# Where a segment's normalised features are made: after the previous segment's last projection, or between its matmuls

## The chip, the cores and the metric

The kernel runs on one core of a Trainium2 chip. A core has five engines with a queue each: TensorE (PE, matrix products; the profile lists its weight loads as PEld), VectorE (DVE), ScalarE (ACT), GpSimd (POOL), and SyncE (SP), which here only issues DMAs. Each engine works through its own queue in order and waits on semaphores for the others. The metric is device time in microseconds (us); smaller is better.

## The reference

The reference is one transformer block with a conditioning vector, in float32. `c` gives six rows of 512 values through `silu(c) @ w_mod`: shift, scale and gate for the attention half, and the same for the feed-forward half.

```
x = A_x                                       # 2048 x 512
h = layernorm(x) * (1 + ca) + sa
x = x + ga * A(h)
h = layernorm(x) * (1 + cb) + sb
x = x + gb * ((h @ w_gate) * (h @ w_up)) @ w_down
```

`A` is attention with 32 heads of 16 and a compressive memory. The 2048 rows are four segments of 512. Inside a segment it is a softmax over the keys at or before the query, with `q = h @ wq`, `k = h @ wk`, `v = h @ wv`. Beside it each head keeps a 16x16 memory `M` and a vector `z` of all earlier segments: the answer of the memory is `phi(q) M / phi(q) z`, with `phi(t) = t + 1` above zero and `exp(t)` below; it is mixed with the softmax part by `sigmoid(beta)`, and after each segment `M` and `z` take in `phi(k)` and `v`. The output goes through `wo`.

## The kernel before

**Numbers as pairs.** Products of float32 matrices are made of three passes: each operand is split into a high part `H` and a low part `L` (what is left over), and PE adds up HH, LH and HL. The splitting costs ACT a copy and another engine a subtraction for every tile.

**The features of a segment.** `ln` (lines 207 to 231) turns the 512 rows of a segment, four tiles `xt[0..3]` of 128 rows, into four column blocks `d = 0..3`, each 128 x 512. It is a generator, and is advanced step by step by whoever calls it. Its steps are, for segments after the first:

- four row steps of `ln_rows` (line 167): `bn_stats` and `bn_aggr` on DVE, one row tile each;
- one step for the reciprocal root: Ln and Exp on ACT (lines 181, 183) and five small operations on POOL (lines 187 to 191);
- four row steps that subtract the mean and multiply, one row tile each, on DVE;
- four feature steps, one per column block: four transposes on PE into a PSUM bank (tile `atp`), ACT scales and shifts that into `ahf` (line 205) and copies it to `ahH` (line 222), POOL subtracts to get `ahL` (line 223). After the second and the fourth of them the generator yields `False`.

**The projections.** `a_kq(s, g, nm)` (line 747) makes keys or queries of one group of eight heads (g = 0..3) of segment s: twelve matmuls into one PSUM bank (`kps` or `qps`), in four quarters of three, quarter k reading feature block k. It yields after each quarter. After the last quarter ACT takes the bank out (`kf`, `qf`, line 765); a chain on ACT and POOL then splits it into three bfloat16 parts (lines 770 to 780) and SP writes them to HBM. Where the memory needs phi, two more ACT passes follow (lines 801, 802).

**The loop and the fill.** From line 1113 a loop runs over 32 units v (four heads of a segment each) in five slots. A slot puts, in this order, into the queues: `q_step` (two PE banks of logits, whose maxima DVE takes), in slot 1 `av_step` (32 matmuls `tb`), then the fill, then `k_step` (logits again, into the one bank pair `lk`, which ACT turns into exponentials, line 330, and POOL masks, line 333). The fill is the work of other stages: the projections, the features, the memory. `fill_a` (line 955) gives its order. PE's instructions are chained in program order, and so are DVE's in the loop; DVE and ACT work that calls `pin` stands behind the PE instruction before it.

How much fill goes into a slot is counted in credit (line 1044): each of the slots 0, 2, 3 and 4 adds 0.25 x 5.8 = 1.45 (5.2 from unit 20 on), slot 1 adds nothing; a quarter of a projection takes 0.68, a feature step 0.45, a row step nothing, a memory step 0.5 or 0.9. The slot's fill ends when the credit is no longer above zero. A `False` ends the slot's fill at once, and what credit is left stays for the next slot.

**Who advances `ln`.** For the next segment, `fill_a` loads the four row tiles at g = 2 (line 975) and weaves the steps of `ln` into the projections of g = 2 and g = 3 (lines 977 to 980). `weave(a, b, at)` (line 669) advances b after the yields of a whose numbers are in `at`: 0, 1, 2 are after the first three quarters, 3 is after the last, with the bank already being emptied or, for queries of later segments, at the first waiting step of the memory. What `ln` has not done by then is done in one go at line 963, before the next segment's first keys.

**Buffers.** Projections and transposes share two PSUM banks (tag "ms"). High and low parts of the features have eight buffers in all, just those of one segment; `ahf` has three. The queries of g = 3 are the last readers of a segment's features: their quarter k is the last use of block k.

Of the kernel before, what the change touches and what calls it, by code (L numbers as in the profile page):

```python
# [58 lines left out]
def tile_kernel(ctx, tc, x, wq, wk_, wv, wo, beta, w_gate, w_up, w_down, c, w_mod, out):  # L59
# [29 lines left out]
    def MM(*a, **k):  # L89
        return pe(nc.tensor.matmul(*a, **k))  # L90
# [12 lines left out]
    def pst(shape, tag, name, dt=F32):  # L103
        tg, n = TAGS[tag]
        return psp.tile(list(shape), dt, tag=tg, name=name, bufs=n)
# [4 lines left out]
    def bank(name, dt=F32, shape=(P, 512)):  # L110

        nbank[0] += 1
        return pst(shape, btag[nbank[0] % len(btag)], name, dt)
# [53 lines left out]
    def ln_rows(pool, xt, s, pfx):  # L167

        first = pfx == "a" and s == 0
        V, A = (CV, CA) if first else (vec, act)  # L170
        mv = pool.tile([P, 4, 2], F32, tag="mv", name=f"{pfx}mv{s}", bufs=2)
        for t in range(4):
            st = pool.tile([P, 6], F32, tag="st", name=f"{pfx}st{s}_{t}", bufs=2)
            i = V.bn_stats(st, xt[t])
            if not first:
                pin(i)
            V.bn_aggr(mv[:, t, :], st)
            if not first:
                yield 0.0
        sd = pool.tile([P, 4], F32, tag="sd", name=f"{pfx}sd{s}", bufs=2)  # L180
        A.activation(sd, mv[:, :, 1], AF.Ln, bias=epst[:, 0:1])
        y = pool.tile([P, 4], F32, tag="y", name=f"{pfx}y{s}", bufs=2)
        A.activation(y, sd, AF.Exp, scale=-0.5)
        a = pool.tile([P, 4], F32, tag="ya", name=f"{pfx}ya{s}", bufs=2)
        b = pool.tile([P, 4], F32, tag="yb", name=f"{pfx}yb{s}", bufs=2)
        eng = CV if first else nc.gpsimd
        eng.tensor_mul(a, y, y)
        eng.tensor_scalar(b, mv[:, :, 1], 1.0, EPS, op0=ALU.mult, op1=ALU.add)
        eng.tensor_mul(b, b, a)
        eng.tensor_scalar(b, b, -0.5, 1.5, op0=ALU.mult, op1=ALU.add)  # L190
        eng.tensor_mul(y, y, b)
        yield 0.0
        for t in range(4):
            i = V.tensor_scalar(xt[t], xt[t], mv[:, t, 0:1], y[:, t:t + 1],
                                op0=ALU.subtract, op1=ALU.mult)
            if not first:
                pin(i)
                yield 0.0
        if first:
            yield 0.0  # L200

    def ln_col(ps, h, xt, d, sc, sh, A):
        for t in range(4):
            TP(ps[:, t * P:(t + 1) * P], xt[t][:, d * P:(d + 1) * P], ident)
        A.activation(h, ps, AF.Identity, scale=sc[:, d:d + 1], bias=sh[:, d:d + 1])

    def ln(pool, hpool, xt, s, sc, sh, pfx, hb, fast, kept_h=None):

        first = pfx == "a" and s == 0
        V, A = (CV, CA) if first else (vec, act)  # L210
        yield from ln_rows(pool, xt, s, pfx)
        hH, hL = [], []
        for d in range(KT):
            h = pool.tile([P, L], F32, tag="hf", name=f"{pfx}hf{s}_{d}", bufs=hb[2])
            ln_col(bank(f"{pfx}tp{s}_{d}"), h, xt, d, sc, sh, A)
            hi = hpool.tile([P, L], F32R, tag=hb[0].format(d), name=f"{pfx}hH{s}_{d}", bufs=hb[1])
            lo = hpool.tile([P, L], F32R, tag=hb[0].format(4 + d), name=f"{pfx}hL{s}_{d}", bufs=hb[1])
            if fast:
                V.tensor_copy(hi, h)
                V.tensor_sub(lo, h, hi.bitcast(F32))  # L220
            else:
                act.activation(hi, h, AF.Copy)
                nc.gpsimd.tensor_sub(lo, h, hi.bitcast(F32))  # L223
            hH.append(hi)
            hL.append(lo)
            if kept_h is not None:
                kept_h.append(h)
            yield 0.45
            if not first and d % 2 == 1:
                yield False  # L230
        return hH, hL

# [37 lines left out]
    def q_step(u, i):  # L270

        Q, K = qst[u % NB], kst[u % NB]
        if i == 0:
            nms[u] = ap.tile([P, 16], F32, tag="nm", name=f"nm{u}", bufs=2)
        nm = nms[u]
        for b in range(2):
# [7 lines left out]
            for hh, qb in parts:  # L284
                n = (qb + 1) * P
                MM(qp[:, c:c + n], Q[0:96, hh, qb * P:(qb + 1) * P], K[0:96, hh, 0:n], start=True, stop=True)
                c += n
# [14 lines left out]
    def n_step(u):  # L302

        Q = qst[u % NB]
        tp = pst([32, P], "tb", f"ntp{u}", BF)
# [3 lines left out]
        for i in range(2):  # L309
            nc.scalar.dma_start(Q[96 + i:97 + i].rearrange("p h (q t) -> p (h q) t", t=P), nt[16 * i:16 * i + 16])  # L310

    def k_step(u, i):

        Q, K = qst[u % NB], kst[u % NB]
        kp = psp.tile([P, 2, 512], F32, tag="lk", name=f"k{u}_{i}", bufs=1)

        def mm(b, c, h, kb):
            MM(kp[:, b, c:c + L - kb * P], K[:, h, kb * P:(kb + 1) * P], Q[:, h, kb * P:], start=True, stop=True)

# [240 lines left out]
    def load_mod(i):  # L560
        r = []
        for k in range(KT):
            a = pa.tile([P, 512], F32, tag="x", name=f"wm{i}_{k}", bufs=4)
            nc.sync.dma_start(a, wm[:, k, i * D:(i + 1) * D])
            r.append(a)
        return r
# [102 lines left out]
    def weave(a, b, at):  # L669

        i = 0
        for w in a:
            yield w
            if w:
                for _ in range(at.count(i)):
                    w = next(b, None)
                    if w or w is False:
                        yield w
                i += 1
# [275 lines left out]
    def fill_a():  # L955
        for w in w2:
            next(w)
        yield from av
        memq.extend((a_mem(0, 0), a_mem(0, 1)))
        lns = None  # L960
        for s in range(NSEG):
            if s > 0:
                hcur[0] = yield from lns
                if s < 3:
                    r = load_mod(2 * s)
            for g in range(2 if s == 0 else 0, NG):
                ws = []
                if s == 0 and g < 3:
                    ws = [load_g(nm, w, g + 1) for nm, w in (("k", wk_), ("q", wq))]
                for w in ws:  # L970
                    next(w)
                K, Q = a_kq(s, g, "k"), a_kq(s, g, "q")
                if g >= 2 and s + 1 < NSEG:
                    if g == 2:
                        xts[s + 1] = xload(s + 1)
                        lns = a_ln(s + 1)
                        Q = weave(Q, lns, (0, 1, 2, 3) if s > 0 else (2, 3))
                    else:
                        K = weave(K, lns, (0, 2) if s > 0 else (0, 1, 2, 3))
                        Q = weave(Q, lns, (0, 1, 2))  # L980
                if g == 1 and 0 < s < 3:
                    acc = mod_acc(r)
                    K, Q = weave(K, acc, (0, 2)), weave(Q, acc, (0, 2))
                if s == NSEG - 1 and g == 1:
                    xr0 = xr_load(0, pa, (0, 1), "x")
                    ready = chain(wo_weights(), wo_op(0, None, B["orl"], us[0]))
                if s == NSEG - 1 and 0 < g < NG - 1:
                    K, Q = weave(K, ready, (0, 1, 2, 3)), weave(Q, ready, (0, 1, 2, 3))
                if s == NSEG - 1 and g == NG - 1:
                    yield from weave(Q, ready, (0, 1, 2, 3))  # L990
                    memq.append(a_mem(s, g))
                    yield from K
                    yield from ready
                    yield from wo_mm(0, us[0], xr0, (0, 1))
                    break
                yield from K
                for w in ws:
                    next(w)
                yield from Q
                if s > 0 and g == 0:  # L1000
                    while vfree[0] < s:
                        yield None
                    if s < 3:
                        yield from weave(a_v(s), mod_acc(r), (1, 3, 5, 7))
                        yield from a_mod(2 * s, r[0])
                        r = load_mod(2 * s + 1)
                    else:
                        yield from a_v(s)
                        B["orl"] = wo_load(0, wpool)
                if g == 1 and 0 < s < 3:  # L1010
                    yield from a_mod(2 * s + 1, r[0])
                memq.append(a_mem(s, g))
        while memq or memt:
            yield mem_step() or 0.0
            yield False
# [283 lines left out]
    for q in range(2):  # L1299
# [98 lines left out]
        for m in range(2):  # L1398
            s = 2 * q + m
# [111 lines left out]
```

## Time and profile before

| | us |
|---|---|
| three timed runs | 879.31, 879.39, 883.21 |
| their median | 879.39 |
| the profiled execution's own time | 881.91 |
| span in that execution, first to last instruction | 879.8 |
| PE busy | 832.8 |
| DVE busy | 650.6 |
| ACT busy | 472.5 |
| POOL busy | 424.1 |

The loop over the 32 units fills about the span from 40 to 500 us; what comes after is the feed-forward half. The three places where one segment's features are made for the next lie at about 80, 195 and 315 us. In a timeline row stand the start, the time from start to end of what is merged in the row, the engine, the line, the operation, its output and inputs, shapes and count; a bracket at the end gives the idle time of the engine before it and what ended it. PE's matmuls overlap, so the distance from one start to the next says more than a length. PE's line is mostly L90, a helper that records every matmul, so one goes by tile names: `k`, `q`, `tb` are the attention, `kps` and `qps` the projections, `atp` the transposes of the features.

### The profile page before, as it was taken

The page shows a single profiled execution, that of the slowest core. Times are in us where ns is not written, and L with a number is a line of the kernel's source. Part 1 is how long each engine was busy: PE and PEld are TensorE (multiplying, and loading weights), DVE is VectorE, ACT ScalarE, POOL GpSimd, SP SyncE. Part 2 cuts the span into 40 slices and gives each one's busy share as a digit, 9 for nine tenths or more (in the row PEclk, how much of TensorE's full clock was granted, in tenths as well). Part 3 has the DMA queues.
Part 4 walks back from the last instruction along what each step waited for, and adds up shares of the span by engine and source line. Part 5 has one row for each costly group of instructions (what it writes and reads, how often), then busy time and mean ns, then how long its engine had stood idle before and what let it go on. Part 6 is the DMA issues. An engine that isn't in the chain of part 4 may idle for free.

```text
span 879.8 us, 14406 instructions
## 1 busy us (share of the span) xinstructions
PE 832.8 (95%) x4824; PEld 583.0 (66%) x4824; DVE 650.6 (74%) x1728; ACT 472.5 (54%) x740; POOL 424.1 (48%) x564
## 2 busy tenths in 40 slices
PE   8998999989999989999978899999999999999998
PEld 5765565555565656655644567788778888887886
DVE  7697677986778868788888759898784856666532
ACT  3757667777677766777554664333363523333321
POOL 4545546546455665486352533987200846550000
PEclk9999899999999999999999999999999999999999
DMA  7774456665648665677695552543414232212032
GB/s 236 225 235 159 146 160 201 214 209 174 207 142 252 199 190 157 220 234 239 209 285 177 160 180 97 176 146 105 163 30 127 87 120 64 56 55 93 0 118 96
DMA packets 112667, 139.46 MB, mean 159 GB/s; under 512 B 20112, under 2 KB 71312, under 8 KB 112592
## 3 DMA queue, kind: packets, MB, share of 16 engines
q1 hardware_dynamic: 106368, 130.91, 48.7%
q10 hardware_dynamic: 6224, 7.62, 2.4%
q8 instruction: 38, 0.62, 0.3%
q14 instruction: 37, 0.30, 0.1%
HBM read 87.48 MB, written 50.76 MB: 157 GB/s over the span
## 4 chain that ended last, share of the span: by engine, by line
PE 66%; DVE 13%; DMA 8%; ACT 5%; POOL 4%; issue 3%; ACTq 1%; SPq 0%; POOLq 0%; DVEq 0%
PE g L90 23%; PE acc L90 14%; PE tb L90 5%; DVE q L40 5%; PE k L90 5%; PE q L90 5%; PE vps L90 4%; PE kps L90 3%; PE qps L90 2%; ACT pt L330 2%; DMA xr<-in_x_dram 2%; PE wops L90 2%; POOL ahL L223 1%; DVE x L40 1%; DVE nm L40 1%
## 5 line engine op out<-in xcount | busy, mean ns | idle before, releaser
L40 DVE CUSTOM_DVE_ANT_0 q<-q,cmask 128x384 f32<-128x384 f32 (+3 forms) x512 | 246.7, 508 | 66.4 <-PE q L90 56.4
L330 ACT ACTIVATE pt<-k 128x1024 f32<-128x1024 f32 x160 | 163.8, 1024 | 68.7 <-PE k L90 47.3
L333 POOL TENSOR_SCALAR_AFFINE_SELECT pt<-pt 128x256 f32<-128x256 f32 (+1 forms) x224 | 105.4, 484 | 174.3 <-ACT pt L330 173.9
L90 PE MATMUL q<-kst,qst 96*128 96x384 bf16 (+3 forms) x512 | 102.1, 301 | 11.7 <-DVE nm L40 10.4
L90 PE MATMUL k<-qst,kst 98*128 98x384 bf16 (+3 forms) x512 | 97.9, 303 | 11.6 <-ACT pt L330 10.7
L448 POOL TENSOR_TENSOR w<-w 128x256 f32<-128x256 f32 (+1 forms) x84 | 72.0, 869 | 55.7 <-DMA w<-in_w_up_dram 38.2
L443 POOL TENSOR_TENSOR AL<-w,AH 128x512 fp32r<-128x512 f32 (+1 forms) x42 | 58.2, 1388 | 48.0 <-ACT AH L439 46.8
L90 PE MATMUL tb<-pt,v 128*32 128x512 f32 (+3 forms) x1024 | 76.2, 438 | 0.2 <-POOL pt L333 0.2
L90 PEld LDWEIGHTS <-kst 98*128 98x128 bf16 x512 | 38.8, 99 | 56.6 <-issue 48.4
L40 DVE DVE_READ_ACCUMULATOR2_ANT nm<- 128x1 f32 x512 | 72.3, 141 | 0.0
L90 PEld LDWEIGHTS <-qst 96*128 96x128 bf16 x512 | 43.6, 98 | 39.1 <-issue 14.4
L439 ACT ACTIVATE AH<-w 128x512 fp32r<-128x512 f32 (+3 forms) x88 | 46.8, 565 | 33.6 <-POOL w L448 20.5
L1453 DVE TENSOR_TENSOR mL<-mid,mH 128x512 fp32r<-128x512 f32 (+1 forms) x44 | 32.9, 751 | 41.4 <-ACT mH L1452 39.4
L90 PE MATMUL acc<-DH,mL 128*128 128x512 f32 x144 | 56.6, 393 | 0.9 <-DVE mL L1453 0.9
L90 PE MATMUL acc<-DH,mH 128*128 128x512 f32 x144 | 57.2, 397 | 0.0
L90 PE MATMUL acc<-DL,mH 128*128 128x512 f32 x144 | 56.5, 393 | 0.0
L90 PEld LDWEIGHTS tb<-pt,v 128*32 128x32 f32 x1024 | 28.7, 110 | 39.5 <-issue 35.9
L1452 ACT ACTIVATE mH<-mid 128x512 fp32r<-128x512 f32 (+1 forms) x44 | 27.1, 627 | 51.7 <-PE acc L90 50.1
L1245 ACT ACTIVATE p<-g 128x512 f32<-128x512 f32 (+1 forms) x22 | 13.1, 597 | 73.2 <-PE g L90 73.1
L443 DVE TENSOR_TENSOR AL<-w,AH 128x512 fp32r<-128x512 f32 (+3 forms) x44 | 29.2, 671 | 19.1 <-ACT AH L439 18.2
L359 ACT ACTIVATE tsb<-tb 128x512 f32<-128x512 f32 x32 | 19.1, 596 | 35.0 <-PE tb L90 33.4
L90 PE MATMUL g<-chH,AH 128*128 128x512 f32 (+1 forms) x88 | 34.8, 395 | 0.7 <-ACT p L1245 0.7
(286 smaller groups left out, 2060.1 us busy)
## 6 DMA issues: line engine op xcount, KB each, us to landing
kst<-kd SPq DMA_DIRECT2D x32, 384.0 KB
qst<-qd SPq DMA_DIRECT2D x32, 384.0 KB
td<-tsb ACTq DMA_DIRECT2D x28, 256.0 KB
wm<-in_w_mod_dram SPq DMA_DIRECT2D x24, 256.0 KB
kd<-k SPq DMA_DIRECT2D x16, 384.0 KB
qd<-q SPq DMA_DIRECT2D x16, 384.0 KB
w<-in_w_gate_dram SPq DMA_DIRECT2D x40, 128.0 KB
w<-in_w_up_dram SPq DMA_DIRECT2D x40, 128.0 KB
```

Of the source, the lines that this page charges most:

```text
L40: i = getattr(self.eng, name)(*a, **k)
L90: return pe(nc.tensor.matmul(*a, **k))
L223: nc.gpsimd.tensor_sub(lo, h, hi.bitcast(F32))
L330: lpt[0] = act.activation(pt, kp, AF.Exp, scale=0.25)
L333: sels[u, i] = nc.gpsimd.affine_select(w, w, pattern=[[0, w.shape[1]], [1, P]], compare_op=ALU.is_ge, fill=0.0, base=0, channel_multiplier=-1)
L359: act.activation(tsbs[u], tbs.pop(u), AF.Copy)
L439: i = act.activation(hi[sl], w[sl], AF.Copy)
L443: i = eng.tensor_sub(lo[sl], w[sl], hi[sl].bitcast(F32))
L448: i = ce.tensor_tensor(w[:, o, :, 0:n], w[:, x, :, 0:n], w[:, y, :, 0:n], op=op)
L1245: lcp[0] = act.activation(r["p1"], ps, AF.Copy)
L1452: pin(act.activation(mH[0:n], md[0:n], AF.Copy))
L1453: vec.tensor_sub(mL[0:n], md[0:n], mH[0:n].bitcast(F32))
```

## The change

Two edits. In `ln` the `False` after every second feature step stays only for the features of the feed-forward half (`pfx == "c"`). And the steps of `ln` are woven elsewhere. In the table, b is a `bn_stats` step, r the reciprocal root, m a subtract-and-multiply step, f a feature step; the place is the projection and the quarter after which it stands.

| | K, g = 2 | Q, g = 2 | K, g = 3 | Q, g = 3 | line 963 |
|---|---|---|---|---|---|
| s = 0 before | | 2 b, 3 b | 0 b, 1 b, 2 r, 3 m | 0 m, 1 m, 2 m | f f, f f |
| s = 0 after | 3 b | 0 b, 1 b, 2 b, 3 r | 1 m, 2 m, 3 m m | 0 f, 1 f, 2 f, 3 f | |
| s > 0 before | | 0 b, 1 b, 2 b, 3 b | 0 r, 2 m | 0 m, 1 m, 2 m | f f, f f |
| s > 0 after | 2 b, 3 b | 0 b, 1 b, 2 r | 0 m, 1 m, 2 m, 3 m | 0 f, 1 f, 2 f, 3 f | |

```diff
             yield 0.45
-            if not first and d % 2 == 1:
+            if pfx == "c" and d % 2 == 1:
                 yield False
...
                     if g == 2:
                         xts[s + 1] = xload(s + 1)
                         lns = a_ln(s + 1)
-                        Q = weave(Q, lns, (0, 1, 2, 3) if s > 0 else (2, 3))
+                        K = weave(K, lns, (2, 3) if s > 0 else (3,))
+                        Q = weave(Q, lns, (0, 1, 2) if s > 0 else (0, 1, 2, 3))
                     else:
-                        K = weave(K, lns, (0, 2) if s > 0 else (0, 1, 2, 3))
-                        Q = weave(Q, lns, (0, 1, 2))
+                        K = weave(K, lns, (0, 1, 2, 3) if s > 0 else (1, 2, 3, 3))
+                        Q = weave(Q, lns, (0, 1, 2, 3))
```

No instruction is added or removed.

## The prediction

> **What bounds the kernel now.** I read the page first, then the waits of the keys' bank `kps`, then PE's timeline around 80, 195 and 315 us, and last the granted clock and the rows of DVE, ACT and POOL there.
>
> ```profile
> span 879.8 us, 14406 instructions
> ...
> PE 832.8 (95%) x4824; PEld 583.0 (66%) x4824; DVE 650.6 (74%) x1728; ACT 472.5 (54%) x740; POOL 424.1 (48%) x564
> ```
>
> ```profile
> PE 66%; DVE 13%; DMA 8%; ACT 5%; POOL 4%; issue 3%; ACTq 1%; SPq 0%; POOLq 0%; DVEq 0%
> ```
>
> ```profile
> its engine sat idle before it (us, times) until:
>   POOL ahL L223: 12.2, 15
> ```
>
> PE is busy or stepping through its queue nearly always, and the chain that ends last is two thirds PE. So a stall of PE's queue in the loop is a stall of the kernel, and work that only fills PE's gaps is free. The keys of a new segment are such a stall: PE and its weight loads sat 12.2 us, in 15 pieces, until POOL had subtracted the low part of a feature block (the two overlap, so I count from start to start instead).
>
> ```profile
> 79.87 1.05 PE L93 MATMUL atp<-ident,x 128*128 128x128 f32 x8
> 80.75 0.60 PE L90 MATMUL k<-qst,kst 98*128 98x384 bf16 x4
> ...
> 82.05 1.10 PE L93 MATMUL atp<-ident,x 128*128 128x128 f32 x8
> 83.40 0.60 PE L90 MATMUL k<-qst,kst 98*128 98x256 bf16 x4 [0.26 <-ACT pt L330]
> 83.83 0.60 PE L90 MATMUL q<-kst,qst 96*128 96x384 bf16 x4
> 85.11 0.50 PE L90 MATMUL kps<-ahH,wkH 128*128 128x512 f32 x1 [0.67 <-ACT ahf L205]
> ...
> 91.53 1.08 PE L90 MATMUL k<-qst,kst 98*128 98x512 bf16 x2
> ...
> 96.17 0.66 PE L93 MATMUL mp<-ident,phk 128*128 128x128 f32 x4
> ...
> 105.75 0.61 PE L90 MATMUL k<-qst,kst 98*128 98x512 bf16 x2
> ...
> 109.02 0.61 PE L90 MATMUL k<-qst,kst 98*128 98x512 bf16 x2
> ```
>
> ```profile
> 88.00:94.00 6.00, 5.82 (x17) 2.75 (x21) 0.90 (x5) 2.15 (x4) 3.10 (x4) 0.50 0.61 189
> 310.00:320.00 10.00, 7.69 (x53) 5.53 (x52) 7.64 (x28) 10.00 (x16) 5.73 (x11) 1.00 0.60 168
> ```
>
> Here segment 1's features stand two by two in two slots (82.05 is the second pair), and all twelve key matmuls follow at once in the next slot. That is the credit: each pair spends 0.90 of 1.45, `False` ends the slot, and the 1.1 left over buys four quarters in one go. ACT and POOL need the time of several slots for four feature blocks, and PE stands. Behind it the granted clock (the column after POOL) is 0.50 for 6 us; around segment 3 it is 1.00.
>
> ```profile
> 179.32 0.39 PE L90 MATMUL qps<-ahH,wqH 128*128 128x512 f32 x1
> ...
> 199.18 0.50 PE L90 MATMUL kps<-ahH,wkH 128*128 128x512 f32 x1
> ...
> 204.05 0.61 PE L90 MATMUL k<-qst,kst 98*128 98x256 bf16 x4
> ...
> 215.51 0.59 PE L90 MATMUL vps<-wvH,ahH 128*128 128x512 f32 x1
> ...
> 217.78 0.61 PE L90 MATMUL k<-qst,kst 98*128 98x256 bf16 x4
> ```
>
> ```profile
> 298.04 0.39 PE L90 MATMUL qps<-ahH,wqH 128*128 128x512 f32 x1
> ...
> 312.42 0.61 PE L93 MATMUL mT<-ident,mem 128*128 128x128 f32 x4
> 314.53 0.60 PE L90 MATMUL k<-qst,kst 98*128 98x384 bf16 x4 [1.50 <-ACT pt L330]
> ...
> 315.40 1.04 PE L93 MATMUL atp<-ident,x 128*128 128x128 f32 x8
> 316.96 0.60 PE L90 MATMUL k<-qst,kst 98*128 98x256 bf16 x4 [0.53 <-ACT pt L330]
> ...
> 317.81 0.48 PE L90 MATMUL kps<-ahH,wkH 128*128 128x512 f32 x1
> ...
> 322.75 0.61 PE L90 MATMUL k<-qst,kst 98*128 98x512 bf16 x2
> ```
>
> **What the change takes away.** Undisturbed measures: nine matmuls of such a projection with the next row's start take 217.78 - 215.51 = 2.27 us, so twelve take 2.27 x 12 / 9 = 3.03; eight transposes take 80.75 - 79.87 = 0.88; from one `k` to the next over slot 1's attention, 109.02 - 105.75 = 3.27; `k` to `q`, 83.83 - 83.40 = 0.43.
>
> Segment 1: transposes 1.35 - 0.88 = 0.47; `q` to the keys 1.28 - 0.43 = 0.85; keys 6.42 - 3.03 = 3.39; the attention behind them, still at half clock, 4.64 - 3.27 = 1.37. Together 6.08. Segment 2: nine key matmuls, 4.87 - 2.27 = 2.60. Segment 3: 2.11 - 0.44 (four transposes) = 1.67, 1.56 - 0.88 = 0.68, keys 4.94 - 3.03 = 1.91; together 4.26. In all **12.9 us**, of which 6 us x 0.5 = 3.0 are the half clock of segment 1. I expect it all to go: with one feature step behind each query quarter (0.68 + 0.45 against 1.45 a slot) the four blocks spread over three to four slots, and the last of them has at least a slot to be copied and subtracted before quarter 3 of the keys wants it. By the credit the first keys are through at the same slot as before, give or take one, since the same sum is spent (queries 4 x 0.68, features 4 x 0.45, keys 4 x 0.68: 7.24, five slots of 1.45): nothing behind them starts sooner by plan. What the change can win is stalls.
>
> **What it costs.** No instruction is new, none costs PE time of its own. The features issue no DMA; only the four `wm` loads behind line 963 move past SP's writes of the queries, by a slot or less, with a slot's time to spare before their use: nothing.
>
> First block. Its transposes need all four m steps, and these now stand just ahead of the queries. DVE runs behind PE:
>
> ```profile
> 71.41 0.55 DVE L40 TENSOR_SCALAR x<-x,amv,ay 128x512 f32<-128x512 f32 x1 [1.95 <-POOL ay L191]
> ```
>
> ```profile
> 70.83 0.49 PE L90 MATMUL qps<-ahH,wqH 128*128 128x512 f32 x1
> ```
>
> ```profile
> 179.25 1.00 DVE L40 TENSOR_SCALAR x<-x,amv,ay 128x512 f32<-128x512 f32 x2
> ...
> 184.47 2.00 DVE L40 TENSOR_SCALAR x<-x,amv,ay 128x512 f32<-128x512 f32 x2
> ```
>
> ```profile
> 299.05 1.46 DVE L40 TENSOR_SCALAR x<-x,amv,ay 128x512 f32<-128x512 f32 x2
> ```
>
> At segment 2 DVE would finish the last two m steps where it did the two of that slot, at 180.25, and PE would want them after the first query quarter, at 179.32: 0.93 us of stall. At segment 3 the slot's maxima hold DVE until 299.05 and one m step takes 0.55, to 299.60; PE is there at 298.04: 1.56. At segment 1 three m steps follow one another once DVE is through with the maxima, at 71.41 - 1.95 = 69.46: with 0.55 each to 71.11, where PE, with a memory product between, comes at 70.83: 0.28. Sum **2.8 us**. The bank for these transposes, emptied by ACT meanwhile, is covered by that wait; without it, it would cost about one eviction, 0.79 by the nearest row below. The ends are 0 (DVE caught up) and 4.8: 2.00 for two is the slowest row, 1.0 more for each of two segments.
>
> [...]
>
> ACT and POOL:
>
> ```profile
> L205 ACT ACTIVATE ahf<-atp,modc x12: 767/788/815, 81.0 to 317.4; 128x512 f32<-128x512 f32 x12
> L222 ACT ACTIVATE ahH<-ahf x12: 632/648/679, 83.2 to 319.5; 128x512 fp32r<-128x512 f32 x12
> L223 POOL TENSOR_TENSOR ahL<-ahf,ahH x12: 1259/1272/1715, 84.2 to 321.1; 128x512 fp32r<-128x512 f32 x12
> ```
>
> ```profile
> L330 ACT ACTIVATE pt<-k 128x1024 f32<-128x1024 f32 x160 | 163.8, 1024 | 68.7 <-PE k L90 47.3
> ...
> L90 PE MATMUL tb<-pt,v 128*32 128x512 f32 (+3 forms) x1024 | 76.2, 438 | 0.2 <-POOL pt L333 0.2
> ```
>
> A slot with one feature gives ACT 1.02 + 0.79 + 0.65 = 2.46 us, while PE needs 0.43 + 0.44 + 0.76 + 0.43 = 2.1 (logits twice, four transposes, a quarter). The splitting of the last keys comes on top, and `lk` is one buffer: PE's next `k` waits for the exponential of the one before. Slot 1 gives time back: 3.27 us of PE with one exponential and one eviction. Before, a pair of features in a slot cost PE 0, 0.47, 0.68 and, a slot later, 1.67 us in the four cases shown here, 0.7 on average. Single ones let ACT through between, but stand among more ACT work; I take 0.5 for two, **3.0 us** for six times two. The ends are 0 and everything exposed, 12 x 1.44 = 17.3 us. POOL's 1.27 us a block now lies beside the key splitting; attention behind POOL waited 0.2 us in the whole run, and I take nothing, at most 1.27 a segment.
>
> Row steps. The b steps stand a projection sooner, nearer to the loads of `x`; if one is late, DVE stands, and the maxima PE waits for are queued behind it. I take 0; a price is the nearest DVE wait, 1.95 us a segment. That very wait, for the reciprocal root at segment 1, should go (a step is left empty there). I count no gain, since PE's waits for DVE in that stretch are those of every slot 1; at most it is 1.95.
>
> **The sum.** -12.9 + 2.8 + 3.0 = -7.1 us; 881.91 - 7.1 = 874.8 against the profiled execution. The median, 879.39, is 2.5 lower, about the 3.0 of one half-clock stretch: its runs may well have had none. Then it is 879.39 less 4.1, 875.3; if they had it, less 7.1, 872.3. Between these, and nearer to the first, I say **874.5**.
>
> **Rivals.**
>
> The half clock stays or comes back (874.5 + 3.0 = 877.5). For it: transposes with waits around them are what stood ahead of it. Against it: the 1.50 us of idle at 314.53, behind transposes too, brought none. [...]
>
> The waits only move (about 879.4): what PE no longer loses at the keys it loses between the queries, at the bank and at `lk`, ACT having the same work. For it: ACT's 2.46 against 2.1. Against it: the stalls at the keys were POOL's, at the end of the chain, and that end is now off PE's path.
>
> The features expose ACT (slower): every `k` behind a feature waits, in all three segments. With everything exposed it is 17.3 + 2.8 - 12.9 = 7.2 us more, 886.6. It turns a loss when over (12.9 - 2.8) / 17.3 = 58% of the features' ACT time is exposed. Against it: slot 1's slack.
>
> **Chances.** Forecast, spread from 868.5 to 876: 0.60, of which 0.52 below 875.0. Clock rival 0.14; moved waits 0.14; exposed ACT 0.12. The low end is the forecast without the 3.0 of ACT on a median that had the half clock, 879.39 - 10.1 = 869.3, and a little under; the high end, 881.5, leaves out most of the last rival. 0.5%, about 4.4 us, is what a measurement of this kernel can tell from no change: faster 0.52, same 0.36, slower 0.12.
>
> **What would show it.** Right: `kps` no longer waits for `ahL`; `atp` stands in fours between quarters of `qps`; the clock stays at 1.00 at 80 to 100 us; small waits of `atp` for DVE's `x`. Wrong: waits of `k` for `pt` or of `atp` for `ahf` that add up to over 5 us, a new stretch at 0.50, `bn_stats` waiting for the loads.

## The result, and the profile after

The changed kernel takes 885.85 us (median of nine runs, 883.95 to 890.50); the kernel before takes 882.66 in runs taken beside them. The ratio is 1.0045, 95% interval 1.0027 to 1.0064: about 0.45% slower. The forecast was 874.5, 0.6% below the 879.39 on record then. That was the median of three runs, and with nine it is 3.3 us higher. The profiled execution took 885.79 us, its span is 883.8, against 881.91 and 879.8 before.

From the page after, and from the groups that read or write `kps`:

```profile
span 883.8 us, 14435 instructions
...
PE 835.3 (95%) x4824; PEld 584.1 (66%) x4824; DVE 654.1 (74%) x1728; ACT 473.3 (54%) x740; POOL 421.7 (48%) x564
```

```profile
its engine sat idle before it (us, times) until:
...
  POOL ahL L223: 3.0, 3
```

Each engine's count of instructions is that of before; the first line counts 29 more in all, of kinds that the profile does not count as work. The stall that the change was to remove, counted over PE and its weight loads, went from 12.2 us to 3.0. PE's timeline after, at segment 1, shows the features where they now stand, one behind each query quarter, and what is left of the wait; the windows (stretch, length, busy us and instructions of PE, PEld, DVE, ACT and POOL, then the clock, DMA's share and GB/s) show that the half clock at 88 us (0.50 before, 1.00 now) is gone and two new stretches have come:

```profile
79.21 0.60 PE L93 MATMUL atp<-ident,x 128*128 128x128 f32 x4
79.56 0.48 PE L90 MATMUL qps<-ahH,wqH 128*128 128x512 f32 x1
...
81.50 0.61 PE L93 MATMUL atp<-ident,x 128*128 128x128 f32 x4
...
83.68 0.60 PE L93 MATMUL atp<-ident,x 128*128 128x128 f32 x4
84.04 0.48 PE L90 MATMUL kps<-ahH,wkH 128*128 128x512 f32 x1
...
89.86 0.50 PE L90 MATMUL kps<-ahL,wkH 128*128 128x512 f32 x1 [1.13 <-POOL ahL L223]
```

```profile
88.00:94.00 6.00, 4.87 (x46) 2.41 (x47) 3.05 (x12) 3.98 (x7) 4.51 (x5) 1.00 0.97 287
...
218.00:222.00 4.00, 3.29 (x20) 0.93 (x23) 3.10 (x16) 0.00 (x0) 0.00 (x0) 0.59 0.53 188
380.00:384.00 4.00, 3.68 (x23) 1.04 (x25) 3.43 (x14) 0.63 (x1) 3.49 (x5) 0.50 0.85 232
```

PE's waits, before and then after, say where the gain went: the queries' banks now wait for DVE's maxima (in each row us in total, times, longest).

```profile
PE k L90 <- ACT pt L330: 10.7, 11, 2.3
PE q L90 <- DVE nm L40: 10.4, 24, 0.9
```

```profile
PE q L90 <- DVE nm L40: 17.2, 27, 2.6
PE k L90 <- ACT pt L330: 8.0, 10, 1.6
```

**A table by units finds the place.** Every pass v of the loop has one run of `tb` matmuls, so the start of its first `tb`, taken from PE's timeline, is a clock for the kernel. Before in us, the others as what they stand later (+) or sooner (-):

| v | before | after | seg1_only | seg2_only | seg3_only | phi_spare | wo_early | phi_wo | paid_late | seg12_phi |
|---|---|---|---|---|---|---|---|---|---|---|
| 1 | 74.15 | +1.18 | +0.07 | -0.11 | -1.11 | +1.20 | -0.14 | +1.32 | -0.43 | +0.56 |
| 3 | 106.73 | -2.14 | -3.26 | +1.30 | -2.24 | -2.13 | -3.46 | -2.01 | -4.62 | -2.76 |
| 8 | 174.74 | -1.83 | -3.27 | +1.29 | -2.26 | -1.84 | -3.15 | -1.81 | -4.14 | -2.45 |
| 9 | 191.24 | -1.33 | -3.31 | +1.76 | -2.26 | -1.37 | -2.66 | -1.33 | +1.69 | -1.98 |
| 10 | 208.06 | -4.51 | -3.31 | -1.41 | -2.26 | -4.39 | -5.81 | -4.48 | -0.47 | -5.13 |
| 11 | 220.94 | -1.33 | -3.31 | +1.55 | -2.28 | -4.28 | -2.84 | -4.37 | -0.47 | -5.02 |
| 12 | 235.06 | -0.65 | -3.31 | +2.37 | -2.26 | -5.09 | -3.38 | -5.17 | -0.47 | -5.83 |
| 16 | 291.60 | +0.40 | -3.56 | +6.27 | -2.13 | -4.06 | -2.35 | -4.15 | +0.32 | -4.71 |
| 17 | 307.23 | +0.94 | -3.56 | +6.34 | -1.09 | -3.51 | -1.80 | -3.60 | +5.42 | -4.63 |
| 21 | 363.14 | +0.21 | -1.92 | +5.97 | -1.81 | -4.24 | -2.50 | -4.30 | +3.70 | -4.60 |
| 22 | 375.51 | +5.36 | -1.93 | +6.21 | +3.46 | -0.05 | -1.52 | -3.33 | +3.67 | -4.56 |
| 31 | 507.31 | +4.56 | +1.77 | +5.68 | +0.40 | +0.15 | -2.29 | -3.59 | +5.01 | -3.30 |

The column "after" has two gains, 3.32 us from unit 1 to 3 (segment 1) and 3.18 from 9 to 10 (segment 2), and two losses that stand at no boundary: 3.18 from unit 10 to 11 and 5.15 from 21 to 22. A single step of the table can also hold work that has moved from one unit to the next: segment 2's 16 transposes stand between units 9 and 10 before, and between 8 and 9 after, so over both steps its gain is 2.68.

**Unit 11.** Timeline after, then before (`...` stands for rows left out):

```profile
213.87 0.61 PE L93 MATMUL mp<-ident,phk 128*128 128x128 f32 x4
...
214.81 0.64 ACT L802 ACTIVATE phq<-qf 128x512 f32<-128x512 f32 x1
...
215.47 0.69 DVE L40 SCALAR_TENSOR_TENSOR phq<-phq,rlq 128x512 f32<-128x512 f32 x1 [2.48 <-ACT phq L802]
...
218.18 0.38 PE L90 MATMUL q<-kst,qst 96*128 96x256 bf16 x2 [2.57 <-DVE nm L40]
...
219.61 3.59 PE L90 MATMUL tb<-pt,v 128*32 128x512 f32 x32
```

```profile
211.23 0.60 PE L93 MATMUL mp<-ident,phk 128*128 128x128 f32 x4
...
217.99 0.62 ACT L802 ACTIVATE phq<-qf 128x512 f32<-128x512 f32 x1
...
220.94 2.36 PE L90 MATMUL tb<-pt,v 128*32 128x512 f32 x32
```

`phq` is the phi of segment 2's first queries, one of three `ph` buffers. Before, it is made 6.8 us behind the transposes `mp` that read segment 1's last `phk`. After, `mp` stands 2.6 us later and the queries are through sooner: ACT makes `phq` 0.94 us behind the start of `mp`, DVE stands 2.48 us for it, PE 2.57 us for the maxima queued behind it on DVE, and the clock falls to 0.50 from 219 to 222 us. Counted in slots from the first `tb` of unit 10, `mp` is in the second slot before and in the fifth after, and these queries end in the third slot before and in the second after.

**Unit 22.** After, then before:

```profile
365.62 2.15 SPq L928 DMA_DIRECT2D wor<-in_wo_dram  x2
...
373.57 2.51 POOL L931 TENSOR_TENSOR wor<-wor,gab 128x512 f32<-128x512 f32 x2 [3.10 <-DMA wor<-in_wo_dram]
...
376.33 0.62 ACT L935 ACTIVATE woH<-wor 128x512 fp32r<-128x512 f32 x1
376.48 0.59 PE L90 MATMUL k<-qst,kst 98*128 98x512 bf16 x2 [1.57 <-ACT pt L330]
...
376.98 1.49 DVE L40 TENSOR_TENSOR woL<-wor,woH 128x512 fp32r<-128x512 f32 x1 [4.43 <-ACT woH L935]
...
379.44 0.59 PE L90 MATMUL q<-kst,qst 96*128 96x256 bf16 x2 [2.37 <-DVE nm L40]
380.87 4.50 PE L90 MATMUL tb<-pt,v 128*32 128x512 f32 x32
```

```profile
363.61 0.99 SPq L928 DMA_DIRECT2D wor<-in_wo_dram  x2
...
370.19 2.54 POOL L931 TENSOR_TENSOR wor<-wor,gab 128x512 f32<-128x512 f32 x2
...
374.29 0.62 ACT L935 ACTIVATE woH<-wor 128x512 fp32r<-128x512 f32 x1
...
375.64 1.33 DVE L40 TENSOR_TENSOR woL<-wor,woH 128x512 fp32r<-128x512 f32 x1
```

The output weights `wo` are loaded and split between segment 3's projections. After, the loads start 2.0 us later and DVE comes to `woL` 3.1 us sooner (376.98 - 4.43 = 372.55 against 375.64): DVE waits for ACT, ACT for POOL, POOL for the load, and PE for DVE and ACT.

### The profile page after: what moved, and what is told of

Its sections match the earlier page's. It is cut to its first block, busy times and chain, and to the rows that moved or that the text cites. A ratio compares the mean times of both kernels' runs of the same rounds, so it can differ in the third digit from the quotient of the medians.

```text
span 883.8 us, 14435 instructions
## 1 busy us (share of the span) xinstructions
PE 835.3 (95%) x4824; PEld 584.1 (66%) x4824; DVE 654.1 (74%) x1728; ACT 473.3 (54%) x740; POOL 421.7 (48%) x564
## 4 chain that ended last, share of the span: by engine, by line
PE 66%; DVE 13%; DMA 8%; ACT 5%; POOL 3%; issue 3%; SPq 1%; ACTq 1%; POOLq 0%; DVEq 0%
PE g L90 23%; PE acc L90 14%; PE tb L90 6%; DVE q L40 5%; PE k L90 5%; PE q L90 4%; PE vps L90 3%; PE kps L90 3%; PE wops L90 2%; ACT pt L330 2%; PE qps L90 2%; PE mz L90 1%; DMA orl<-od 1%; DVE x L40 1%; DMA x1d<-xr 1%
## 5 line engine op out<-in xcount | busy, mean ns | idle before, releaser
L90 PE MATMUL q<-kst,qst 96*128 96x384 bf16 (+3 forms) x512 | 102.9, 302 | 18.7 <-DVE nm L40 17.2
L90 PE MATMUL tb<-pt,v 128*32 128x512 f32 (+3 forms) x1024 | 78.9, 450 | 0.0
L443 DVE TENSOR_TENSOR AL<-w,AH 128x512 fp32r<-128x512 f32 (+3 forms) x44 | 29.3, 672 | 19.2 <-ACT AH L439 18.3
```

The source lines that it names most:

```text
L443: i = eng.tensor_sub(lo[sl], w[sl], hi[sl].bitcast(F32))
```

## The experiments

Theory "late followers": the boundary stalls went as meant, but the order of all work behind a boundary moved, projections ahead of memory steps, until it met the old order again, and the losses are two followers that came too late in it. Rivals: the features cost ACT at each boundary; the half clock makes the difference.

**One boundary at a time.** The new lists and the missing `False` for the features of one segment alone. Against the kernel before, for segment 1 (for 2 and 3 the numbers in `s in (...)` differ):

```diff
-            if not first and d % 2 == 1:
+            if (pfx == "c" or s in (2, 3)) and d % 2 == 1:
...
-                        Q = weave(Q, lns, (0, 1, 2, 3) if s > 0 else (2, 3))
+                        if s in (0,):
+                            K = weave(K, lns, (2, 3) if s > 0 else (3,))
+                            Q = weave(Q, lns, (0, 1, 2) if s > 0 else (0, 1, 2, 3))
+                        else:
+                            Q = weave(Q, lns, (0, 1, 2, 3) if s > 0 else (2, 3))
```

(and the same for g = 3).

> The new places of the row and feature steps hold for segment 1's features alone; segments 2 and 3 are made as before. Theory 'late followers' (the stalls ahead of the keys go, and what is lost in the changed kernel comes later, from work that the shifted order brings too late): the step before unit 2's first tb is shorter by 3.4 us as in the changed kernel, PE's order is the old one from then on, nothing is lost behind it: 3.4 us below before, ratio 0.996. Rival 'features cost ACT at each boundary': a third of the changed kernel's loss, ratio 1.001 to 1.002. Rival 'half clock' (the time follows how many stretches at 0.50 a run has): below before only if the stretch at 88 us is gone.

> The new places for segment 2's features alone. Late followers: 3.2 us gained at unit 10, 3.2 lost at unit 11, where the phi of segment 2's first queries waits for a buffer that the late transposes of the memory (mp) hold, some tenths won and 0.8 lost up to unit 16, as in the changed kernel between unit 9 (-1.33) and unit 16 (+0.40): +1 to +2 us against before, ratio 1.001 to 1.002. Features cost ACT: the same size, but then the loss stands at waits of k for pt between the query quarters (190 to 205 us), not at 213 to 219 us.

> The new places for segment 3's features alone. Late followers: nothing won at units 15 to 18, 1.5 us lost at unit 19, and some 5 at unit 22, where the low part of wo waits for late loads: +3.5 to +5 us against before, ratio 1.004 to 1.006, most of the changed kernel's loss. Features cost ACT: +1 us, in units 16 to 18. Half clock: no more than before, unless a stretch at 0.50 appears.

Measured against before: segment 1 alone 0.9993 (0.9972 to 1.0015), segment 2 alone 1.0050 (1.0029 to 1.0072), segment 3 alone 1.0047 (1.0026 to 1.0068). The table has each step where the theory put it: segment 1 alone gains 3.33 us up to unit 3 and loses nothing right behind; segment 2 alone gains 3.17 at unit 10 and loses 2.96 at unit 11; segment 3 alone loses 5.27 at unit 22 and is level from 16 to 21. Segment 3 alone shows the same wait:

```profile
375.08 1.49 DVE L40 TENSOR_TENSOR woL<-wor,woH 128x512 fp32r<-128x512 f32 x1 [4.55 <-ACT woH L935]
```

The size failed for segment 1: its runs are not 0.4% faster, though a step of 3.3 us is in its trace. Its trace has the clock down in three other places (319 to 323, 476 to 483, 489 to 497 us, with means of 0.57, 0.51 and 0.57), and over its twelve runs the mean granted clock is that of before, 0.990. So the stretch at 88 us went, and the runs as a whole had no less of it. Segment 2 alone is above its forecast of 1.001 to 1.002. Its trace loses 3.90 us from unit 12 to 16, with a stretch at half clock at 288 to 296 us that no other trace has, and its twelve runs have a mean granted clock of 0.986 against 0.990, so less clock goes with a part of it; what brings it there is open. The three ratios add up to some 0.9%, twice the whole change's 0.45%; with some 0.2% to either side of each, what one boundary costs is not known better than to about 2 us.

**The phi buffer.** In the changed kernel:

```diff
-                e = pa.tile([P, L], F32, tag="ph", name=f"ph{nm}{s}_{g}", bufs=3)
+                if nm == "q" and g == 0 and s > 1:
+                    e = wpool.tile([P, L], F32, tag="orl", name=f"ph{nm}{s}_{g}", bufs=4)
+                else:
+                    e = pa.tile([P, L], F32, tag="ph", name=f"ph{nm}{s}_{g}", bufs=3)
```

> The changed kernel, with the phi tiles of the first queries of segments 2 and 3 in a buffer of wpool (tag orl) that nothing else uses at that time, instead of the third ph buffer. Late followers: ACT's phq no longer waits for mp; DVE's 2.48 us at 215 and 0.99 us at 334 go, PE's 2.57 us at 218 with them, and so does the stretch at half clock at 219: 3.2 + 1 us below the changed kernel, about 881.5. If phq is late for another reason (its place in ACT's queue, its input qf), nothing changes: 885.9.

881.18 us, 0.9991 of before (0.9969 to 1.0013). Segment 2's `phq` is now made ahead of `mp`, nobody waits for it, and unit 11 keeps its gain (-4.28 against -1.33):

```profile
210.87 0.63 ACT L805 ACTIVATE phq<-qf 128x512 f32<-128x512 f32 x1
...
212.97 0.69 DVE L40 SCALAR_TENSOR_TENSOR phq<-phq,rlq 128x512 f32<-128x512 f32 x1
...
213.99 0.61 PE L93 MATMUL mp<-ident,phk 128*128 128x128 f32 x4
```

So what held `phq` at unit 11 was the buffer. The half clock at 218 us is gone from this trace too: the 32 `tb` of unit 11 take 2.36 us, 3.59 in the changed kernel. The same wait at segment 3 (DVE's 0.99 us at 334) stayed, against the expectation, and with it the 1.5 us at unit 19 (5.23 sooner than before at unit 18, 3.73 at 19). With both mends of the next part it reads:

```profile
329.35 0.93 DVE L40 SCALAR_TENSOR_TENSOR phq<-phq,rlq 128x512 f32<-128x512 f32 x1 [0.99 <-ACT phq L805]
```

```profile
331.85 0.38 PE L90 MATMUL q<-kst,qst 96*128 96x256 bf16 x2 [0.56 <-DVE nm L40]
332.76 0.38 PE L90 MATMUL q<-kst,qst 96*128 96x256 bf16 x2 [0.53 <-DVE nm L40]
```

Here `phq` has the spare buffer, and ACT makes it behind an exponential, `q` and `rlq`, without a gap from 326.73 us on. So the buffer is not what holds this third late follower; what does, no run here tests.

**The loads of wo, and both.** The first two loads go ahead of segment 3's values, to 324 us:

```diff
-        raw = {}
+        raw = B["raw"]
...
+            if k not in raw:
...
+                        B["raw"] = {}
+                        for k in range(2):
+                            B["raw"][k] = wpool.tile([P, D], F32, tag="wor", name=f"wor{k}", bufs=2)
+                            pin(nc.sync.dma_start(B["raw"][k], wo[k * P:(k + 1) * P, :]))
                         yield from a_v(s)
```

> The changed kernel, with the loads of the first two blocks of wo issued ahead of segment 3's values, some 30 us sooner. Late followers: POOL's first scaling no longer waits 3.10 us for them, DVE's woL not 4.43 us, PE's k and q not 1.57 and 2.37 us; the step from unit 21's tb to unit 22's goes from 5.15 us longer than before to at most 1 longer: 4 to 5 us below the changed kernel, 881 to 882. If the wait comes from POOL's or ACT's own queue instead, the step stays.

> The changed kernel with both: the spare phi buffer and the early loads of wo. Late followers: both steps go; from the traces 3.3 us won at segment 1, 3.2 at segment 2, nothing at segment 3 and nothing lost at units 11 and 22: 4 us below before, 877 to 878, ratio 0.995. If the losses only move on once more (another late follower, or the half clock), it stays at 881 to 882, the time of before.

> The kernel before with the same spare phi buffer and early loads of wo, and the features where they were. Neither wait is in its trace, so no theory expects a gain: within 1 us of before. If it is as much below before as the changed kernel with both is, the features' place wins nothing.

`wo_early` takes 879.81 us, 0.9988 (0.9964 to 1.0013), a little below its forecast; its step at unit 22 is 0.98 us and DVE's wait 0.51, while the loss at unit 11 (2.97) is all there:

```profile
370.35 1.45 DVE L40 TENSOR_TENSOR woL<-wor,woH 128x512 fp32r<-128x512 f32 x1 [0.51 <-ACT woH L936]
...
373.99 2.36 PE L90 MATMUL tb<-pt,v 128*32 128x512 f32 x32
```

With both mends 878.66 us, 0.9969 (0.9948 to 0.9990): faster than before and than the changed kernel, by less than the 4 us expected. The kernel before with both mends is at 1.0002 (0.9981 to 1.0024): they win nothing by themselves, so what the pair wins is the new place of the features and row steps. PE's wait for the maxima, 17.2 us in the changed kernel, is 10.5 with both mends, as before. In the runs each mend alone takes some 0.55% off the changed kernel's 1.0045, and both together 0.76%: less than the sum, but within the intervals.

**The half clock as a rival.** `wo_early` has the wait at unit 11 without a stretch behind it, and loses 2.97 us there, against 3.18 with the stretch. So the wait is the loss at unit 11. The stretch itself shows in the next unit: from 11 to 12 the changed kernel loses 0.68 and `wo_early` wins 0.54, some 1.2 us apart. At unit 22 no trace has the wait without a stretch (there `tb` takes 4.50 us in the changed kernel, 4.05 in `phi_spare` and 3.56 in `seg3_only`, against 2.36 in `wo_early`).

**The row steps alone.** The features back behind the last queries with their `False`; the row steps stay sooner.

```diff
-            if pfx == "c" and d % 2 == 1:
+            if not first and d % 2 == 1:
...
-                        Q = weave(Q, lns, (0, 1, 2, 3))
```

(the second for g = 3.)

> Only the row steps sooner; the features stand where they were, behind the last queries, two by two with the end of the slot after each pair. No fill moves on PE except by the order of the row steps, so the waits of the keys for ahL stay (12 us), the orders meet again after each boundary, and neither late phi nor late wo appears: within 1 us of before by the late followers. If the row steps themselves are what is lost (DVE's m steps ahead of the maxima), 2 to 3 us above before.

> The kernel with the row steps sooner alone, a second time: its trace stood 1.6 us below before at the end of the loop, its runs 0.3% above. If the row steps cost something, again 0.1 to 0.5% above; if the first set was the spread of the half-clock stretches, within 0.1% of before.

1.0031 (1.0006 to 1.0055), then 1.0012 (0.9990 to 1.0034). The first is 2.3 us above before, as the rival on the row steps had it; the second is at the lower end of its forecast for a cost (0.1 to 0.5%), and its interval holds none as well. In neither trace is the loop longer (1.55 and 3.36 us sooner at unit 31), and in the first PE waits 10.6 us for the maxima, as before (10.4). But both profiled runs were among the fastest of their sets, and both sets have a little less clock (0.989 and 0.988 against 0.990). No follower is late; whether the row steps cost some tenths of a per cent stays open.

**The old order back.** If the moved order is the cause, it must go when a feature step counts nothing where it stands, and is paid for where it stood:

```diff
-            yield 0.45
+            yield 0.0 if pfx == "a" else 0.45
...
                 hcur[0] = yield from lns
+                for w in (0.45, 0.45, False, 0.45, 0.45, False):
+                    yield w
```

> The changed kernel, but a feature step counts nothing in the credit where it now stands; its 0.45 is counted where the features stood before (two times two, each pair ended by False). Then every projection, value and memory step behind a boundary is in the slot where it was before the change, with no new buffer and no load moved. Late followers: the steps at units 11 and 22 go, and the boundaries keep some 3 us at segments 1 and 2: 2 to 4 us below before, ratio 0.995 to 0.998. Features cost ACT: the features now stand on top of full slots, k waits for pt and atp for ahf there by 3 us or more, and the time is that of before or above.

> The same with the spare phi buffer and the early loads of wo. Late followers: with the order of before nothing is late, so these two win nothing: as paid_late, within 1 us. If something is still late in paid_late, this is below it by that.

885.71 us, 1.0039 (1.0020 to 1.0059), and 886.79, 1.0067 (1.0040 to 1.0094) with both mends. The place was right and the time wrong. In each unit from 8 to 24 PE has the same matmuls of the fill as before again, but for the transposes of the features. Units 11 and 22 lose nothing now, with no buffer and no load changed (from unit 10 to 11 -0.47 and -0.47, from 21 to 22 +3.70 and +3.67), and the mends win nothing more: the order is what made the two followers late. But units 9 and 17 now lose 5.83 and 5.10, where the features of segments 2 and 3 stand on top of full slots. Some 1.8 us of each are the 16 transposes, which have moved into these units (16 x 0.11, by the prediction's 0.88 for eight), and 2.16 and 1.75 come back at units 10 and 18; 3.67 from unit 8 to 10 and 3.35 from 16 to 18 stay lost. At unit 9 PE waits for ACT (first fence), and the windows fit that: ACT is busy 12.87 of 14 us, 92% (second fence), against 13.68 of 16, 86%, in the changed kernel (third). A stretch at half clock (188 to 196 us, 0.50 from 190 to 194) follows in this trace.

```profile
180.73 0.66 PE L93 MATMUL atp<-ident,x 128*128 128x128 f32 x4 [0.83 <-ACT ahf L205]
...
186.17 0.73 PE L90 MATMUL up<-MZ,phq 128*128 128x136 f32 x4 [1.66 <-ACT us L867]
187.75 1.38 PE L90 MATMUL mz<-v,pkr 128*128 128x136 f32 x8 [0.85 <-ACT us L867]
```

```profile
174.00:188.00 14.00, 10.53 (x61) 7.16 (x61) 7.38 (x24) 12.87 (x22) 10.93 (x12) 1.00 0.58 195
```

```profile
172.00:188.00 16.00, 14.51 (x104) 8.86 (x102) 13.98 (x45) 13.68 (x23) 10.68 (x13) 1.00 0.67 207
```

I read this so: the credit that the features take in the changed kernel buys ACT time, and the moved order is its price. The rival on ACT fits this denser form; the change itself shows no such loss (PE's `k` waits less for `pt` than before, 8.0 against 10.7 us).

**Without segment 3.** The new places for segments 1 and 2 (`s in (0, 1)`), with the spare phi buffer:

> The new places for segments 1 and 2 alone, with the spare phi buffer; segment 3 as before, the loads of wo as before. Late followers: the table by units of the kernel with both mends stands at -5.3 at unit 13 and loses 1.7 up to unit 24; with segment 3's old order nothing is lost there: 4 to 5 us below before, ratio 0.994 to 0.996. If segment 3's new place wins something after all, it is above the kernel with both mends.

878.12 us, 0.9970 (0.9950 to 0.9989): the same as with both mends, and somewhat above its forecast. From unit 16 to 21, where segment 3's features are made, the old place loses 0.11 us on before (-4.71 to -4.60) and the new one with both mends gains 0.15 (-4.15 to -4.30): the new place wins nothing there that could be told.

## Why the prediction was wrong

The step that failed is what the prediction drew from the credit: "nothing behind them starts sooner by plan". The sum of the credit was right, and segment 2's keys came one slot sooner, within its "give or take one". But the order behind them moved. The features now lie inside the last queries, so the memory steps that are queued behind those queries come later (the `mp` of unit 11 three slots), and the next projections run ahead of them; the two orders meet again only several units on. In that stretch the three phi buffers and the loads of `wo` had too little slack. The forecast had looked only at what stood at the boundary. The change of each column over stretches of the table:

| from unit to unit | after | with both mends |
|---|---|---|
| 1 to 3 | -3.32 | -3.33 |
| 3 to 8 | +0.31 | +0.20 |
| 8 to 16 | +2.23 | -2.34 |
| 16 to 21 | -0.19 | -0.15 |
| 21 to 22 | +5.15 | +0.97 |
| 22 to 31 | -0.80 | -0.26 |
| together | +3.38 | -4.91 |

So in these traces the late phi, with the half clock behind it, cost 2.23 + 2.34 = 4.6 us and the late `wo` 5.15 - 0.97 = 4.2: a gain of 4.9 became a loss of 3.4. The medians of the runs differ by 885.85 - 882.66 = 3.2; with both mends the runs are 2.8 us below before, less than the 4.9 of that one trace.

The terms one by one:

- **Stalls removed, 12.9.** "I expect it all to go" was too much: most of the keys' wait went (12.2 to 3.0 us), but at segment 1 PE still stands 0.57 us for `ahH` at 88.00 and 1.13 for `ahL` at 89.86, so the last block had not the slot's time that was counted on. In time, segment 1 won 3.3 from unit 1 to 3, against 6.08 - 0.28 - 1.0 = 4.8. The half clock there was over-priced too: the traces that keep the old place have 32.5 to 34.0 us from unit 1 to 3 with that stretch and 31.5 without it (`seg3_only`, `rows_only_again`), the new place 29.3. So it cost 1.1 to 2.5 us, not 3.0, probably since PE would have waited in part of it anyway.
- **Segment 2** won more: 2.34 us from unit 8 to 16 with both mends, against 2.60 - 0.93 - 1.0 = 0.7. Its wait for DVE was about half of the 0.93, and ACT's 1.0 is not seen.
- **Segment 3** won nothing, against 4.26 - 1.56 - 1.0 = 1.7. With both mends it stands 1.16 us better from unit 16 to 18, and the third late follower takes 1.52 at unit 19. In effect that is the rival "the waits only move", but the wait that took the gain is for the maxima behind `phq`, not at the bank or at `lk`.
- **The first block's wait for DVE** was about right in sum: PE's weight loads for these transposes wait 2.5 us in four pieces, against 2.8 (0.22 at segment 1, 0.16 and 0.32 at segment 2, 1.80 at segment 3). That segment 3 has 1.57 us between PE's matmuls (first fence) where 1.56 was forecast is luck in the parts: PE came 0.9 us later than forecast, DVE began 0.4 later, and the m step took 0.99 us instead of 0.55, beside a subtraction on POOL (second and third fence). The step ends 0.28 us after POOL's; whether POOL is what made it longer, no run here shows. The upper end of 4.8 us was not reached.

```profile
300.50 0.33 PE L93 MATMUL atp<-ident,x 128*128 128x128 f32 x1 [1.57 <-DVE x L40]
```

```profile
299.45 0.99 DVE L40 TENSOR_SCALAR x<-x,amv,ay 128x512 f32<-128x512 f32 x1
```

```profile
299.01 1.15 POOL L771 TENSOR_TENSOR kr<-kf,k 128x512 f32<-128x512 f32 x1
```

- **ACT, 3.0.** Not seen as such: `k` waits less for `pt` (8.0 against 10.7 us). That features can expose ACT is seen in `paid_late`.
- **DMAs at nothing.** "A slot's time to spare" was worked out for the `wm` loads. The `wo` loads, five units further down the same fill, were not looked at: that is where the late `wo` came from.
- **The rival on the clock** was half right: the stretch left 88 us, and others came behind the two new waits.

## What to carry to other kernels

Where a planner hands out slots by credit, moving a step moves everything behind it until the orders meet again: list both orders of the fill up to that point, and look at each buffer and load there for its slack (before, by the rows above: 6.2 us for the phi buffer, from the end of `mp` at 211.83 to `phq` at 217.99, and 0.7 for `wo`, from ACT's end at 374.91 to DVE's start at 375.64), not only at the place of the change. Where instructions are chained in program order, as DVE's are here, one late operand is a wait of all that is queued behind it (DVE's 2.48 us for one `phq` became 2.57 us of PE). And a loss found at such a follower can be cheap to mend: here one spare buffer and one earlier load turned 0.45% slower into 0.3% faster.

## What the runs showed of the hardware

In the changed kernel the clock fell to 0.50 behind waits of PE shorter than the stretch it then took: behind 2.57 us at 218 us (0.50 from 219 to 222), and behind 1.57 and 2.37 us at 376 and 379 (0.50 from 380 to 385). The traces without the wait have no such stretch there (`phi_spare` at 218, `wo_early` at 380), but the wait does not always bring it: `wo_early` waits the same 2.56 us at 217 and stays at 1.00 (below). Nor do these two waits stand behind most stretches: `seg1_only` has neither wait, and its trace has three stretches.

```profile
216.00:222.00 6.00, 4.59 (x45) 2.04 (x44) 3.96 (x19) 1.06 (x3) 0.17 (x1) 1.00 0.47 158
```

Cut into windows of 1 us, the lost clock of a stretch (the sum of one minus the clock) came out as 1.7 us or a multiple of it (1.7, 3.4, 5.1, 8.5) in the ten traces cut so: `before` and `after` over the whole span, but for its very end, and `wo_early`, `phi_wo`, `before_phi_wo`, the two of the row steps, the two with the old order back and `seg12_phi` up to 600 us. What sets this size, and why the same wait brings a stretch in one run and none in the next, no run here shows.

Such stretches go with much of the spread of a kernel's runs: the kernel before took 876.87 to 886.92 us in 35 runs, longer where the mean granted clock was lower (correlation -0.75), and the lost clock of these ten traces adds up to 2 to 17 us in each. A gain of 3 us in one trace's loop (`seg1_only`) can so be invisible in twelve runs.
